# Reordering the opening norms of an attention and MLP kernel: tile 3's norm ahead of tile 4's statistics, half of tile 2's statistics between the first two norms

## The chip, the cores and the metric

The kernel runs on one core of one Trainium2 chip. The metric is the device time of one execution in microseconds (us). The span of a trace is some 1.8 us shorter than the time of the same execution.

## The reference, cut to what matters

```
x = A_x                                  # 2048 tokens x 1024, bf16
xn = layernorm(x)
s = attention(xn, wqkv, wo)              # 32 heads of 32
y = layernorm(xn)
g = silu(gelu(y @ w1 + b1) @ w2 + b2)
return x + s * g
```

The 2048 tokens are 16 tiles of 128. Below, PE is the engine for matmuls (TensorE), ACT is ScalarE, DVE is VectorE and POOL is GpSimd; PEld is PE's loading of weights. Before any matmul of use can start, a tile of `x` must be loaded, its mean and variance computed, the tile normalized, and the result transposed. The change concerns this opening alone.

## The kernel before

Every operation goes through a small helper, `op`, that records what it reads and writes and derives the semaphores. An engine executes its own operations in the order in which they were recorded, so the order of the calls below is the schedule.

```
load_x(0); load_x(1)
load_wq(0, (1,))                 # key weights, 512 KB
load_x(2); load_x(3)
load_wq(0, (0,))                 # query weights
load_x(4); load_x(5)
load_wq(0, (2,))                 # value weights
... the other tiles

def stat(tb):                    # DVE: two halves of 512 columns, then their merge
    bn_half(tb, 0); bn_half(tb, 1); bn_merge(tb)

def rstd(lo, hi):                # var + eps, then ** -0.5
    op("vector" if hi == 1 else "gpsimd", ... tensor_scalar(L(0), mv[:, lo:hi, 1], EPS, None, op0=ALU.add) ...)
    op("gpsimd", ... tensor_tensor(L(2), L(0), mhalf[:, 0:hi - lo], op=ALU.pow) ...)

def xnorm(tb): ...               # DVE: (x - mean) * rstd, 128x1024 bf16

def norm_pair(p):
    lo, hi = 2 * p, 2 * p + 2
    if p == 0:
        stat(0); rstd(0, 1)
        stat_scalar(1)           # tile 1's statistics, on ACT
        xnorm(0); xnorm(1)
        stat(2); rstd(2, 3)
        stat(3)
        xnorm(2)
        rstd(3, 4)
    elif p == 1:
        stat(4)
        xnorm(3)                 # tile 3's norm, behind tile 4's statistics
        stat(5); rstd(4, 6)
    else: ...                    # stat, two norms, stat, rstd
```

PE's order in the opening is: warm-up matmuls, transposes of tiles 0 and 1 (line L386), key and query matmuls of this first pair (L687), transposes of tiles 2 and 3, value matmuls of the first pair (L703), then the first scores (L867) and, on ACT, the first exponential (L879). A pair is two tiles, the first pair tiles 0 and 1. From the fourth pair on the transposes are done by DMA (tiles 6 to 15).

The softmax here doesn't subtract the row's maximum and nothing guards it: scores larger than these inputs give would overflow.

## Time and profile before

| | before |
|---|---|
| median of 6 runs | 1090.66 us (1089.76 to 1091.55) |
| profiled span | 1087.7 us |
| PE busy | 1077.0 us |
| first exponential starts | 16.19 us |
| first matmul of the body (L395) | 47.92 us |

These are two lines of the page of the kernel before, its busy time by engine and its chain of waits by engine:

```profile
PE 1077.0 (99%) x29156; PEld 700.9 (64%) x29156; DVE 627.3 (58%) x1395; ACT 1043.5 (96%) x1197; POOL 22.6 (2%) x70
PE 54%; ACT 44%; DVE 1%; DMA 0%; issue 0%; POOL 0%; SPq 0%
```

### The profile page before, as it was taken

What the parts mean: (1) busy time and instruction counts of PE and PEld (TensorE: products, weight loads), DVE (VectorE), ACT (ScalarE), POOL (GpSimd) and SP (SyncE); (2) the same over time, 40 slices, a digit from 0 to 9 for tenths busy, and PEclk for the clock granted to TensorE, in tenths of its full rate; (3) what the DMA queues carried; (4) which work ended last, traced back from release to release, by engine and by line L of the source; (5) the groups of instructions that cost most, each with busy time, mean ns of one, the idle gap of its engine ahead of it and who ended that gap; (6) DMA issues with size and microseconds to landing.
All of it is one profiled execution on the core that took longest, in us unless ns stands there. A gap on an engine that the chain in (4) does not pass through costs nothing.

```text
span 1087.7 us, 61820 instructions
## 1 busy us (share of the span) xinstructions
PE 1077.0 (99%) x29156; PEld 700.9 (64%) x29156; DVE 627.3 (58%) x1395; ACT 1043.5 (96%) x1197; POOL 22.6 (2%) x70
## 2 busy tenths in 40 slices
PE   8999999999999999999999999999999999999998
PEld 5766666666666666666666666666666666666665
DVE  7388843477732576642377743378733377635556
ACT  7899998999999999999999999999999999999993
POOL 4400000000000000000000000000000000000000
PEclk9999999999999999999999999999999999999999
DMA  8844365423364224345333264423254333675434
GB/s 247 169 139 137 111 172 149 121 61 110 109 164 122 65 63 120 109 104 148 90 100 100 69 161 119 125 81 109 81 132 119 91 119 108 198 201 107 108 92 124
DMA packets 209336, 131.92 MB, mean 121 GB/s; under 512 B 52538, under 2 KB 200250, under 8 KB 209082
## 3 DMA queue, kind: packets, MB, share of 16 engines
q1 hardware_dynamic: 209082, 127.97, 42.8%
q8 instruction: 228, 3.74, 1.4%
q14 instruction: 26, 0.21, 0.1%
HBM read 104.87 MB, written 12.06 MB: 107 GB/s over the span
## 4 chain that ended last, share of the span: by engine, by line
PE 54%; ACT 44%; DVE 1%; DMA 0%; issue 0%; POOL 0%; SPq 0%
ACT P L879 40%; PE ps L395 32%; PE ps L867 9%; PE ps L896 5%; PE ps L899 5%; ACT u L565 4%; PE ps L703 1%; PE ps L687 1%; ACT thz L609 0%; DVE stats L324 0%; DMA OT<-in_A_x_dram 0%; DVE wq L669 0%; PE ps L386 0%; DVE hT L359 0%; ACT hT L714 0%
## 5 line engine op out<-in xcount | busy, mean ns | idle before, releaser
L879 ACT ACTIVATE P<-ps 128x1024 bf16<-128x1024 f32 x1024 | 968.7, 1085 | 8.6 <-PE ps L867 4.0
L896 PE MATMUL ps<-P,VP 128*32 128x256 bf16 x4096 | 256.3, 273 | 0.0
L899 PE MATMUL ps<-P,ones 128*32 128x256 bf16 x4096 | 256.2, 273 | 0.0
L395 PE MATMUL ps<-yTc,war 128*32 128x352 bf16 (+1 forms) x5376 | 225.3, 309 | 0.0
L395 PE MATMUL ps<-hT,war 128*32 128x352 bf16 (+1 forms) x5376 | 225.2, 309 | 0.0
L867 PE MATMUL ps<-QT,KT 32*128 32x256 bf16 x4096 | 203.4, 273 | 2.9 <-ACT P L879 0.2
L395 PEld LDWEIGHTS ps<-hT,war 128*32 128x32 bf16 x5376 | 127.9, 96 | 73.9 <-issue 25.1
L395 PEld LDWEIGHTS ps<-yTc,war 128*32 128x32 bf16 x5376 | 127.4, 96 | 74.2 <-DVE xb L548 19.0
L867 PEld LDWEIGHTS ps<-QT,KT 32*128 32x128 bf16 x4096 | 60.7, 92 | 114.9 <-issue 60.0
L605 DVE TENSOR_SCALAR zh<-ps,b2h 128x352 f32<-128x352 f32 (+1 forms) x48 | 27.5, 572 | 182.3 <-PE ps L395 182.3
L571 DVE SCALAR_TENSOR_TENSOR hT<-u,xb 128x352 bf16<-128x352 f32 (+1 forms) x168 | 84.4, 510 | 68.4 <-ACT u L565 68.4
L548 DVE TENSOR_SCALAR xb<-ps,b1T 128x352 f32<-128x352 f32 (+1 forms) x168 | 96.3, 573 | 47.7 <-PE ps L395 42.8
L896 PEld LDWEIGHTS ps<-P,VP 128*32 128x32 bf16 x4096 | 109.1, 97 | 20.4 <-issue 1.3
L899 PEld LDWEIGHTS ps<-P,ones 128*32 128x32 bf16 x4096 | 109.2, 97 | 18.7
L395 PE MATMUL ps<-xnT,wq 128*32 128x352 bf16 (+1 forms) x2688 | 112.7, 309 | 0.0
L395 PEld LDWEIGHTS ps<-xnT,wq 128*32 128x32 bf16 x2688 | 63.7, 96 | 37.2 <-DVE xb L548 9.1
L558 DVE SCALAR_TENSOR_TENSOR u<-u,xb 128x352 f32<-128x352 f32 (+1 forms) x168 | 82.6, 510 | 1.9
L554 DVE TENSOR_TENSOR u<-xb 128x352 f32<-128x352 f32 (+1 forms) x168 | 82.6, 508 | 0.7
L565 ACT ACTIVATE u<-u 128x704 f32<-128x704 f32 (+1 forms) x84 | 71.9, 861 | 0.0
L395 PE MATMUL ps<-xnT,OT 128*32 128x352 bf16 (+2 forms) x1568 | 62.9, 306 | 0.2 <-DVE wq L669 0.2
L395 PE MATMUL ps<-wq,xnT 128*32 128x256 bf16 x1536 | 50.8, 274 | 0.0
L395 PEld LDWEIGHTS ps<-xnT,OT 128*32 128x32 bf16 x1568 | 37.7, 96 | 19.9 <-DVE wq L669 7.7
(61 smaller groups left out, 477.6 us busy)
## 6 DMA issues: line engine op xcount, KB each, us to landing
war<-in_B_w_dram SPq DMA_DIRECT2D x336, 256.0 KB, 3.3
wq<-in_A_wqkv_dram SPq DMA_DIRECT2D x36, 128.0 KB, 2.4
OT<-in_A_x_dram SPq DMA_DIRECT2D x16, 256.0 KB, 5.5
xnT<-in_A_x_dram SPq DMA_DIRECT2D x16, 256.0 KB, 3.2
out_dram<-wq SPq DMA_DIRECT2D x15, 256.0 KB, 2.0
y_scratch<-OT SPq DMA_DIRECT2D x14, 256.0 KB, 2.6
gT_scratch<-gst SPq DMA_DIRECT2D x32, 88.0 KB, 3.1
xnT<-in_A_wo_dram SPq DMA_DIRECT2D x8, 256.0 KB, 3.9
```

Source lines behind the costliest of these rows:

```text
L395: ins = e.matmul(outs(j), lhsT=lhs(j), rhs=rhs, start=start, stop=stop, tile_position=(0, 32 * j), skip_group_check=True)
L548: x0 = op("vector", lambda e: e.tensor_scalar(xb[:, 0:n], bank(bk, 0, n), b1T[:, f:f + 1], None, op0=ALU.add), r=[("b", bk), "b1"], w=[kx] ...
L554: x = op("vector", lambda e: e.tensor_tensor(ub[:, 0:n], xb[:, 0:n], xb[:, 0:n], op=ALU.mult), r=[kx], w=[ku], c=151 + 1.042 * n)
L558: x = op("vector", lambda e: e.scalar_tensor_tensor(ub[:, 0:n], ub[:, 0:n], 1.0 / 0.044715, xb[:, 0:n], op0=ALU.add, op1=ALU.mult), r=[kx, ...
L565: x = op("scalar", lambda e: e.activation(ut[:, :, 0:n], ut[:, :, 0:n], ACT.Tanh, scale=0.7978845608028654 * 0.044715), r=kus, w=kus, c=48 ...
L571: op("vector", lambda e: e.scalar_tensor_tensor(hT[:, fq, 0:n], ut[:, i, 0:n], 1.0, xq[:, 0:n], op0=ALU.add, op1=ALU.mult), r=[kus[i], kq] ...
L605: x0 = op("vector", lambda e: e.tensor_scalar(zh[:, 0:n], bank(bk, 0, n), 0.25, b2h[:, nb:nb + 1], op0=ALU.mult, op1=ALU.add), r=[("b", bk ...
L687: ins = e.matmul(bank(bk, off, off + 256), lhsT=wq[:, which, dc, 0:128], rhs=xnT[:, dc, t0:t0 + 256], start=dc == 0, stop=dc == DC - 1, sk ...
L867: ins = e.matmul(bank(bks[j], kh * 256, (kh + 1) * 256), lhsT=KT[i2][32 * j:32 * j + 32, k0:k0 + 128], rhs=QT[i2][32 * j:32 * j + 32, qb * ...
L879: op("scalar", lambda e, p=p, sl=sl: e.activation(pb[:, 2 * p:2 * p + 2, :, :].rearrange("p a b q -> p (a b q)"), ps[:, sl * 1024:(sl + 1) ...
L896: e.matmul(bankq(ACC, j, 0, QW), lhsT=VP[vp][:, kb, vo + 32 * j:vo + 32 * j + 32], rhs=pb[:, j, kh, :], start=first, stop=False, tile_posi ...
L899: ins = e.matmul(bankq(ACC, j, QW, 2 * QW), lhsT=ones[:, 0:32], rhs=pb[:, j, kh, :], start=False, stop=last, tile_position=(0, 32 * j), sk ...
```

## The change

The intent is to have tile 3 normalized before PE wants to transpose it. Tile 4's statistics move behind that norm. Half of tile 2's statistics fills a gap of DVE between norms 0 and 1, for which tile 2 has to be loaded earlier. A small step of tile 3's moves from GpSimd to DVE.

```diff
         load_x(1)
+        load_x(2)
         load_wq(0, (1,))
-        load_x(2)
         load_x(3)
...
-            op("vector" if hi == 1 else "gpsimd", ...
+            op("vector" if hi in (1, 4) else "gpsimd", ...
...
                 xnorm(0)
+                bn_half(2, 0)
                 xnorm(1)
-                stat(2)
+                bn_half(2, 1)
+                bn_merge(2)
                 rstd(2, 3)
                 stat(3)
+                rstd(3, 4)
                 xnorm(2)
-                rstd(3, 4)
+                xnorm(3)
             elif p == 1:
                 stat(4)
-                xnorm(3)
                 stat(5)
```

More of the change, by code (lines that the diff above doesn't have):

```diff
@@ L337, in rstd @@
             L = lambda k: lnp[:, k, lo:hi]
-            op("vector" if hi == 1 else "gpsimd", lambda e: e.tensor_scalar(L(0), mv[:, lo:hi, 1], EPS, None, op0=ALU.add),
+            op("vector" if hi in (1, 4) else "gpsimd", lambda e: e.tensor_scalar(L(0), mv[:, lo:hi, 1], EPS, None, op0=ALU.add),
                r=[("mv", t) for t in range(lo, hi)], w=[("l0", t) for t in range(lo, hi)], c=169.0)
```

## The prediction

> **What bounds the kernel now.** I began with the page: PE is busy for 1077.0 of 1087.7 us and ACT for 1043.5, and the chain that ended last is PE 54% and ACT 44%, DVE 1%. So nothing on DVE matters in the body of the kernel. The diff, however, only touches the prologue (loads, norms of tiles 0 to 3), and there the limits are different. So I read next the chain of waits in order of time from 0 to 60 us:
>
> ```profile
> 7.60 0.55 DVE hT L359
> 8.15 1.21 DVE stats L324 x2
> 9.35 0.02 issue
> 9.38 0.21 DVE mv L328
> 9.59 1.16 DVE stats L324 x2
> ...
> 10.98 0.41 DVE hT L359
> 11.39 1.21 DVE stats L324 x2
> 12.60 0.02 issue
> 12.62 0.21 DVE mv L328
> 12.83 0.42 DVE hT L359
> 13.25 0.05 issue
> 13.30 0.62 PE ps L386 x8
> 13.92 1.75 PE ps L703 x16
> 15.66 0.33 PE ps L867 x8
> ```
>
> Read it as one sentence: from 7.60 to 13.30 us the end of the kernel hangs on DVE, which does tile 1's norm, the statistics of tiles 2 and 3, tile 2's norm, **the statistics of tile 4**, and only then tile 3's norm; that releases tile 3's transposes on PE (L386), the value matmuls (L703) and the first scores (L867). From 13.30 to 56.3 us the chain stays on PE, then alternates with ACT. So a microsecond taken off before 13.30 should shift all that follows, unless something with its own clock (a load) comes in.
>
> How large is the hole? The timeline of PE, ACT and DVE from 10 to 16 us shows it. These are rows of that answer (start, us, engine and line, what; in brackets the idle time before and what ended it):
>
> ```profile
> 11.70 0.61 PE L386 MATMUL ps<-ident,hT 128*128 128x128 bf16 x8
> ...
> 11.90 0.38 ACT L693 ACTIVATE KT<-ps 128x256 bf16<-128x256 f32 x1 [2.01 <-PE ps L687]
> ...
> 12.18 0.38 ACT L693 ACTIVATE QT<-ps 128x256 bf16<-128x256 f32 x1
> ...
> 13.30 0.62 PE L386 MATMUL ps<-ident,hT 128*128 128x128 bf16 x8 [0.99 <-DVE hT L359]
> ```
>
> PE finished tile 2's transposes at 12.31, then sat 0.99 us until tile 3's norm. It is PE's only such gap after the key/query matmuls of the first pair began at 9.94. Its length caps most of what the change can win.
>
> **What the Trainium skill says.** (1) "Perfetto Trace Analysis", section "DMA Instruction — HWDGE (DVE, Sync)": a DMA's bar in the profile ends when the issuing sequencer is done; the movement is not in it. So I take starts plus the "to landing" figure, and the trace agrees: the 0.39 us bar of tile 0's load at 0.72 lands 2.9 later, 3.62, and DVE starts on it at 3.65. (2) "Runtime: NRT & Kernel Launch", section "Instruction fetch mechanics": instructions are refilled by DMA in blocks of 16 KiB, 256 instructions. The trace agrees: PE's 29156 + 29156 instructions over 256 are 227.8, and the page counts 228 packets in its "instruction" queue. (3) "DMA: Bandwidth & Descriptors", section "Queues, rings and completion order": each DMA engine takes turns between queues, and a load's completion needs every engine it uses. That makes rival B below possible. (4) "VectorE: DVE Perf Modes", section "The DRAIN you can't avoid": a DVE instruction is not free even where it waits for nothing. The trace agrees in kind: statistics of a tile take 1.32 us from start to start of the aggregation, that 0.12 more, a norm 0.41 to 0.46.
>
> **The change, part by part.** No arithmetic is added or removed, and PE and ACT keep their order.
> - *Tile 2's load ahead of the key weights.* Now tile 2 is issued at 2.11 and lands 5.6 later, 7.7 us. Put third, it follows tile 1 (landed 4.19) with 256 KB; the later 256 KB loads landed some 0.7 apart (7.7, 8.33), so I estimate 5.0. The key weights (issue 1.64 + 5.3 = 6.94 now) go to about 7.7. The query weights have the same bytes ahead of them as before: 3.21 + 6.6 = 9.81, against a use at 9.94. So the first matmuls stay at 9.94, but with only 0.13 to spare.
> - *Half of tile 2's statistics into the gap between norms 0 and 1.* DVE is idle for 1.00 us before 7.60, waiting for GpSimd's power of tile 1. Norm 0 starts at 6.06, so the half (0.66) can run from 6.5 to 7.2 with the load long there. It is free; norm 1 stays at 7.60. DVE is then 0.65 ahead.
> - *Tile 3's first scalar step on DVE instead of GpSimd.* 0.15 on DVE (the row of L338 on DVE) in place of 0.41 on GpSimd, which that instance took beside a DVE norm (0.22 elsewhere).
> - *Norm 3 ahead of the statistics of tile 4.* New DVE times: norm 1 7.60, second half 8.05, aggregation 8.71, statistics of tile 3 from 8.83, aggregation 10.10 to 10.31, scalar step to 10.50; GpSimd's power (0.56, starting 0.09 after) to 11.14. Norm 2 runs 10.45 to 10.95, norm 3 waits for the power, 11.17 to 11.67. That is 1.58 ahead of 12.75, of which PE can use less: PE is in the key/query matmuls until 11.66, so tile 2's transposes stay at 11.70, and tile 3's follow at once, at about 12.15 (a pair of tiles takes 0.89 on the chain, one 0.45) in place of 13.30.
> - *The next limit.* The value matmuls now start at 13.75. They could start at 12.60, but need the value weights (issue 6.25 + 6.4 = 12.65) and a bank that the query copy leaves at 12.56. So about 12.70: **a gain of 1.05 us**, and the first scores at 14.55.
> - *Given back on DVE.* The 0.3 us that DVE waits for the power before norm 3 and the 0.12 of the scalar step come off its lead, so statistics of tile 5 end only some 0.2 us earlier than now, and so do norms 4 and 5 (15.78 and 16.2, against 15.98). PE wants them at 16.5 and 17.0: they still fit. All later norms are also only 0.2 earlier, while PE wants them 1.05 earlier.
>
> Sum, if nothing else intervenes: 1090.87 - 1.05 = 1089.8.
>
> **Rivals.**
> A, *the gain passes through whole*. For it: each later unit of the prologue is 4.48 us on PE, ACT has 0.38 spare in each, and DVE needs only 3.7 per unit. Transposed tiles 6 and 7 land at 23.0 and 24.4, for a use at 24.9; tiles 14 and 15 at 42.2, for one at 42.9. 1089.8.
> B, *a transpose by DMA takes over*. Tile 9's was issued at 25.19 and took 5.1 to landing, where others take 2.7 to 3.9, so it landed at 30.3; PE took the data at 30.43:
>
> ```profile
> xnT<-hT SPq DMA_TRANSPOSE x1, 5.1
> ```
> ```profile
> PEld ps L687 <- DMA xnT<-hT: 0.2, 1, 0.2
> ```
> The reason is in the packets: at 27.55 one 16 KB instruction fetch lay in front of the last part of this transpose on one engine, and that engine trickled until 29.3 at 10 GB/s. Its norm comes only 0.2 earlier after the change. If the landing stays at 30.1, unit 4 starts no earlier than 30.2 and nearly all is lost: 1090.6. Against it: the fetch follows PE's own progress, so it should come 1.05 earlier too, at 26.5, where it still meets this transpose; I expect part of the delay to move with it, and a loss of 0 to 0.8.
> C, *the load order costs something*: query weights after 9.94 would push PE's first pair and subtract one for one. Same bytes ahead of them, so I give it 0.1 on average.
> D, *nothing follows, because the body is bound elsewhere*. The chain after 56 us alternates PE and ACT with no wait on a load that has its own clock (loads are issued behind PE), so a shift should last to the end. The instruction order of later DVE work is fixed by a timing model inside the kernel's builder; a shift of its start can swap a few of them, some tenths either way.
>
> **Range and chances.** A gets about 45%, B 45% with a mean loss of 0.5, the rest small: an expected gain of 0.75 us, 1090.1. The three runs before span 1.8 us, so medians differ by some 0.6 by chance alone; with B's spread that gives 1089.0 to 1091.1 for 8 in 10. 2% is 22 us, more than the whole stretch between 7.6 and 30 us; neither a win nor a loss of that size has a source here: 0.01 each.
>
> **What would show it.** Right: no gap on PE at 12.3; tile 3's transposes near 12.15, value matmuls near 12.7, first scores near 14.5, first exponential near 15.1 in place of 16.19; one half statistic on DVE between the first two norms; norm 3 waiting about 0.3 for GpSimd. For B: a gap on PE before the key matmuls of unit 4 at 29.4, with a DMA as releaser. Wrong: PE's first key matmuls later than 9.94, tile 2's half still waiting for its load at 6.5, norms 4 or 5 holding PE at 16.5, or a start of the body (the first L395, 47.92 now) earlier by one microsecond with an end that is not.

## The result, and the profile after

The changed kernel took 1089.78 us (median of 6 runs, 1088.58 to 1090.78), the kernel before 1090.66 in the same rounds. The ratio is 0.999 with a 95% interval of 0.9977 to 1.0003. Ratios are the mean time of one kernel's fast runs over the mean of the other's of the same rounds, so not quite the ratio of the medians. By times alone the gain isn't separated from zero. The traces separate it in the opening. PE and ACT execute the same sequence in both kernels, and DVE does from tile 5's statistics on, so each step of one trace can be set against the same step of the other.

The two lines of the page that answer to those of before:

```profile
PE 1077.7 (99%) x29156; PEld 701.4 (65%) x29156; DVE 627.6 (58%) x1396; ACT 1043.6 (96%) x1197; POOL 22.5 (2%) x69
PE 57%; ACT 42%; DVE 0%; DMA 0%; issue 0%; POOL 0%; SPq 0%
```

DVE's share of the chain went from 1% to 0%. The chain of waits in order of time (start, duration, what) shows where it went:

```profile
7.52 0.56 DVE hT L359
...
8.12 0.62 PE ps L386 x8
8.74 1.08 PE ps L758 x5
...
9.86 1.92 PE ps L687 x16
11.78 0.89 PE ps L386 x16
...
12.68 1.92 PE ps L703 x16
14.60 0.33 PE ps L869 x8
```

The chain leaves DVE with norm 1, at 8.07 instead of 13.25, and the transposes of tiles 2 and 3 follow each other as one block of 16. The lines are numbered two higher from L756 on, as the changed kernel has two lines more.

DVE's own timeline (the kernel after; in brackets the idle time before an instruction and what ended it):

```profile
6.29 0.69 DVE L324 BATCH_NORM_STATS2 stats<-OT 128x6 f32<-128x512 bf16 x1
7.52 0.55 DVE L359 TENSOR_SCALAR hT<-OT,mv,lnp 128x1024 bf16<-128x1024 bf16 x1 [0.54 <-POOL lnp L717]
...
10.33 0.15 DVE L338 TENSOR_SCALAR lnp<-mv 128x1 f32<-128x1 f32 x1
10.40 0.54 DVE L359 TENSOR_SCALAR hT<-OT,mv,lnp 128x1024 bf16<-128x1024 bf16 x1
11.39 0.55 DVE L359 TENSOR_SCALAR hT<-OT,mv,lnp 128x1024 bf16<-128x1024 bf16 x1 [0.45 <-POOL lnp L340]
...
16.08 0.96 DVE L359 TENSOR_SCALAR hT<-OT,mv,lnp 128x1024 bf16<-128x1024 bf16 x2
```

The half of tile 2's statistics (6.29) sits in the gap and still leaves 0.54 us of it. Norm 3 (11.39) follows norm 2, with 0.45 us of waiting for GpSimd's power. Norms 4 and 5 (16.08) come no earlier than before (15.98).

What PE waits for next is in the weight load ahead of the value matmuls:

```profile
12.68 1.64 PEld L703 LDWEIGHTS ps<-wq,xnT 128*128 128x128 bf16 x16 [0.18 <-DMA wq<-in_A_wqkv_dram]
```

The value weights, landed at 12.64, are the new limit. First exponential 15.13 (before 16.19), body start 46.86 (before 47.92): 1.06 us earlier, both.

Set against the trace before, exponential by exponential, this lead is 1.06 us without a change from 14.6 to 418 us. Between 418 and 426 us it falls to 0.62, and from 438 us to the end it is 0.76, which is the difference of the two spans but for rounding (1087.7 - 1086.9). So 0.3 us was lost in the body. There PE stopped in the middle of one item:

```profile
417.24 0.73 PE L395 MATMUL ps<-yTc,war 128*32 128x320 bf16 x16 [0.51 <-issue]
```

PE's releaser is not named ("issue"), and no semaphore of a load is waited for there: PE first waits for the weights that were being loaded then at 423.7. The place of the stop tells what it was. As the prediction read from the packet count, PE's instructions come by DMA in fetches of 256, each one packet of the "instruction" queue. Counted in PE's instructions from the start of the trace (matmuls, weight loads and semaphore waits), the stop lies after 21441, which is 83 x 256 + 193, and 83 fetches had begun by then. The last of them had begun at 413.87, 1.8 us after PE passed the place 256 instructions earlier (the median over all traces is 0.6), and took 1.90 us (median 1.03). PE went on 1.47 us after its end.

The same count fits every stop of PE over 0.22 us between 60 and 1000 us in the 14 traces: 12 of 12 lie 193 or 194 past a multiple of 256, always with the block of the last begun fetch next. And at the 2898 such places behind the 20th fetch, PE never went on sooner than 1.1 us after the end of that fetch; counted one instruction earlier, it did so 24 times. So PE was out of instructions. Below this is called a fetch stop.

### The profile page after: what moved, and what is told of

Same layout as the page of the kernel before. It is cut to its first block, busy times and chain, and to the rows that moved or that the text cites. A ratio compares the mean times of both kernels' runs of the same rounds, so it can differ in the third digit from the quotient of the medians.

```text
span 1086.9 us, 61820 instructions
## 1 busy us (share of the span) xinstructions
PE 1077.7 (99%) x29156; PEld 701.4 (65%) x29156; DVE 627.6 (58%) x1396; ACT 1043.6 (96%) x1197; POOL 22.5 (2%) x69
## 3 DMA queue, kind: packets, MB, share of 16 engines
HBM read 104.87 MB, written 12.06 MB: 108 GB/s over the span
## 4 chain that ended last, share of the span: by engine, by line
PE 57%; ACT 42%; DVE 0%; DMA 0%; issue 0%; POOL 0%; SPq 0%
ACT P L881 38%; PE ps L395 33%; PE ps L869 9%; PE ps L898 6%; PE ps L901 6%; ACT u L565 3%; PE ps L687 1%; PE ps L703 1%; ACT thz L609 0%; DMA OT<-in_A_x_dram 0%; PE ps L386 0%; DVE wq L669 0%; ACT hT L714 0%; DVE zh L605 0%; DVE wq L671 0%
## 5 line engine op out<-in xcount | busy, mean ns | idle before, releaser
L395 PE MATMUL ps<-yTc,war 128*32 128x352 bf16 (+1 forms) x5376 | 225.5, 309 | 0.5 <-issue 0.5
L395 PE MATMUL ps<-hT,war 128*32 128x352 bf16 (+1 forms) x5376 | 225.3, 309 | 0.0
L395 PEld LDWEIGHTS ps<-yTc,war 128*32 128x32 bf16 x5376 | 127.4, 96 | 74.9 <-DVE xb L548 19.2
L395 PEld LDWEIGHTS ps<-hT,war 128*32 128x32 bf16 x5376 | 127.9, 96 | 73.9 <-issue 25.1
L395 PE MATMUL ps<-xnT,wq 128*32 128x352 bf16 (+1 forms) x2688 | 112.7, 309 | 0.0
L395 PEld LDWEIGHTS ps<-xnT,wq 128*32 128x32 bf16 x2688 | 63.7, 96 | 37.2 <-DVE xb L548 9.1
L395 PE MATMUL ps<-xnT,OT 128*32 128x352 bf16 (+2 forms) x1568 | 62.9, 306 | 0.2 <-DVE wq L669 0.2
L395 PE MATMUL ps<-wq,xnT 128*32 128x256 bf16 x1536 | 50.8, 274 | 0.0
L395 PEld LDWEIGHTS ps<-xnT,OT 128*32 128x32 bf16 x1568 | 37.7, 96 | 19.9 <-DVE wq L669 7.7
```

The lines of the kernel that those rows point to most:

```text
L395: ins = e.matmul(outs(j), lhsT=lhs(j), rhs=rhs, start=start, stop=stop, tile_position=(0, 32 * j), skip_group_check=True)
```

## The experiments

Theory S, behind the prediction: each part of the change frees DVE time ahead of tile 3's norm, and PE's need caps the sum at 1.06 us. Rival O: the order of the norms does everything, and the load and the half are idle extras. Two more questions are what the instruction fetch does (rival B of the prediction), and what the body does with the lead. "Body start" below is the first L395. Experiments e1 to e5 and f3 are single executions of unknown state (e3 and e5 twice); the granted clock was 0.999 or 1.000 in each trace. Only steps of their traces are compared, not their times (1089.1 to 1091.3 us).

**e1: the order alone.**

```diff
                 stat(3)
+                rstd(3, 4)
                 xnorm(2)
-                rstd(3, 4)
+                xnorm(3)
             elif p == 1:
                 stat(4)
-                xnorm(3)
                 stat(5)
```

> Kernel before with one thing of the change: tile 3's power and norm ahead of tile 4's statistics (loads as before, statistics of tile 2 in one piece, scalar step of tile 3 on GpSimd). Theory S (each part frees DVE time, PE's need caps the sum at 1.06): norm 3 at about 12.15 (GpSimd's two steps end only then), tile 3's transposes 12.7, value matmuls at 13.1, first L395 of the body at 47.3, so 0.6 of the 1.06 us. Rival O (the order alone does everything, load and half are idle extras): value matmuls at 12.7, body 1.06 earlier.

Measured: norm 3 at 12.28, value matmuls at 13.34, body start 47.70. That is 0.41 us ahead at the value matmuls, and only 0.22 ahead at the body. Two rows of DVE (e1), norm 3 and norms 4 with 5:

```profile
12.28 0.55 DVE L359 TENSOR_SCALAR hT<-OT,mv,lnp 128x1024 bf16<-128x1024 bf16 x1 [0.84 <-POOL lnp L340]
...
16.97 0.97 DVE L359 TENSOR_SCALAR hT<-OT,mv,lnp 128x1024 bf16<-128x1024 bf16 x2
```

The order alone makes DVE stand for 0.84 us before norm 3, waiting for GpSimd, and everything behind it pays: norms 4 and 5 come 1.0 us later than in the kernel before (15.98), so the transposes of tiles 4 and 5 move only from 17.68 to 17.54. Rival O falls, and theory S, which expected 0.6 at the body, overlooked this cost. By the fifth pair the lead is down to 0.22 us: its key matmuls start at 30.21, just after tile 9's transpose landed at 30.16.

**e2: the load and the half alone.**

```diff
+        load_x(2)
         load_wq(0, (1,))
-        load_x(2)
...
                 xnorm(0)
+                bn_half(2, 0)
                 xnorm(1)
-                stat(2)
+                bn_half(2, 1)
+                bn_merge(2)
```

> Kernel before with the other part: tile 2's load third and half of its statistics between norms 0 and 1; norm 3 stays behind tile 4's statistics. Theory S: all of DVE 0.65 to 0.7 us earlier from norm 2 on, norm 3 at 12.1, transposes 12.6, value matmuls 13.05, body start about 0.65 to 0.7 earlier than before. Rival O: body start unchanged (within 0.1).

Measured: value matmuls at 13.43, body start 47.59, a lead of 0.32 and 0.33 us. Half of what was expected, for a reason that I hadn't seen: tile 4's statistics were now ahead of their own data. The rows of DVE (e2):

```profile
10.97 1.29 DVE L324 BATCH_NORM_STATS2 stats<-OT 128x6 f32<-128x512 bf16 x2 [0.21 <-DMA OT<-in_A_x_dram]
...
12.42 0.49 DVE L359 TENSOR_SCALAR hT<-OT,mv,lnp 128x1024 bf16<-128x1024 bf16 x1
```

Norm 2 came 0.62 us earlier (10.27), norm 3 only 0.33, as tile 4 landed at 10.95 in this execution. The two parts alone add up to 0.22 + 0.33 = 0.55 at the body, together they give 1.06. But part of e2's shortfall is chance of this execution. In the first trace of the changed kernel tile 4 landed at 10.48; with that, its statistics could have begun at 10.68 (norm 2 at 10.27 plus 0.41) in place of 10.97, and e2's lead would be about 0.6 and the sum about 0.8. This is an estimate. What remains is shown by e1: alone, the order makes DVE wait for GpSimd, and the half of the statistics pays for that wait. The order also takes norm 3 out from behind tile 4's load where that is late.

**e3: the scalar step back on GpSimd, twice.**

```diff
-            op("vector" if hi in (1, 4) else "gpsimd", ...
+            op("vector" if hi == 1 else "gpsimd", ...
```

> Changed kernel with tile 3's scalar step back on GpSimd. Theory S: the step takes 0.4 there, beside norm 2, so norm 3 starts at about 11.5 in place of 11.39 and ends at 12.0, still ahead of PE's need at 12.15: value matmuls stay at 12.68, body start within 0.1 of the changed kernel's 46.86. Rival (norm 3 is the bound in the changed kernel): value matmuls later by the same 0.1 to 0.3.

> Tile 3's scalar step on GpSimd again: in the first run of it norm 3 came at 11.68 and tile 3's transposes at 12.28, but the value weights landed at 13.2 (12.6 to 12.8 in most runs) and held PE. With weights landing by 12.7 the value matmuls start at 12.7 to 12.8, 0.1 at most behind the changed kernel's, and body start at 46.9 to 47.0: the scalar step's place is worth at most 0.1. Rival: they start at 13.2 again although the weights are there.

Measured: norm 3 at 11.68 and 11.75, 0.3 later than in the changed kernel, tile 3's transposes at 12.28 and 12.35. The value matmuls came at 13.25 and 13.32, but in both executions they waited for the value weights, which landed at 13.2 and 13.3 (body start 47.42 and 47.49). The question is therefore not answered by a run. Worked out: a block of eight transposes takes 0.45, so with weights at 12.64, as in the changed kernel, PE could have gone on at 12.28 + 0.45 = 12.73, against 12.68. That the step's place is worth under 0.1 us is an estimate, and holds only where the weights land no earlier than that.

**e4: tile 2's load back behind the key weights, the half still in the gap.**

```diff
-        load_x(2)
         load_wq(0, (1,))
+        load_x(2)
```

> Changed kernel with tile 2's load back behind the key weights, the half of its statistics still between norms 0 and 1. The load lands at 7.67, so DVE would hold norm 1 behind it: half 7.7 to 8.35, norm 1 at 8.3 in place of 7.52, first key matmuls at about 10.65 in place of 9.86, body start about 47.6, 0.75 later than the changed kernel and 0.3 earlier than before. Rival (the load's place does not matter): norm 1 at 7.5 and body start 46.9.

Measured, from the rows of DVE (e4):

```profile
7.94 0.69 DVE L324 BATCH_NORM_STATS2 stats<-OT 128x6 f32<-128x512 bf16 x1 [1.52 <-DMA OT<-in_A_x_dram]
8.55 0.53 DVE L359 TENSOR_SCALAR hT<-OT,mv,lnp 128x1024 bf16<-128x1024 bf16 x1
```

DVE is in order, so it stood 1.52 us for tile 2, with tile 1's norm ready behind it. Norm 1 moved from 7.52 to 8.55, the first key matmuls from 9.86 to 10.88, body start to 47.80: 0.94 later than the changed kernel and 0.12 ahead of the kernel before. The load's place is needed, and it cost 0.2 more than expected because the load landed at 7.92.

**f3: the same warm-up in more instructions.** PE warms up with 13 matmuls of 512 columns. Cut into 52 of 128, it has as many columns, but 78 more instructions (39 matmuls, 39 weight loads), so later instruction fetches come earlier.

```diff
-            for i in range(k):
-                ins = e.matmul(bank(0), lhsT=ident[:], rhs=cold, ...)
+            parts = 4 if k == 13 else 1
+            w = 512 // parts
+            for i in range(k * parts):
+                ins = e.matmul(bank(0, 0, w), lhsT=ident[:], rhs=cold[:, 0:4 // parts, :], ...)
```

> Changed kernel; the 13 warm-up matmuls of 512 columns cut into 52 of 128, so 78 more PE instructions in the same PE time. Theory of the fetch (16 KB instruction fetches follow PE's instruction count and hold back one engine's share of the transpose that is under way): the second fetch comes 3 us earlier, at about 22.7 in place of 25.74, into tile 7's transpose (22.9 to 23.9), which then lands at 26 to 26.7 in place of 24.5; PE waits for it ahead of the key matmuls of the fourth pair (24.9 otherwise) for 1 to 1.8 us, and the body starts that much later than 46.86. Rival (fetches don't matter, late landings are chance): tile 7 lands at 24.5, no gap, body start 46.9.

Measured: the opening matched the changed kernel (value matmuls 12.59), and then PE stopped ahead of the fourth pair's key matmuls, as expected, though for less time:

```profile
25.34 1.92 PE L687 MATMUL ps<-xnT,wq 128*128 128x256 bf16 x16 [0.49 <-DMA xnT<-hT]
```

The fetch came at 20.87, earlier than expected, and met tile 6's transpose: that landed at 23.77 (23.11 in the changed kernel), tile 7's behind it at 25.29 (24.52). Body start 47.30, 0.44 later than the changed kernel. Nothing else was altered. This one execution isn't alone: of the transposes of tiles 6 to 9 in all 14 traces, the 24 that had a PE fetch begin while they were under way took 3.51 to 5.11 us from issue to landing, the other 32 took 2.70 to 2.87. Tile 6 met a fetch in f3 only (3.51, against 2.81 to 2.82 in the other 13), and there tiles 8 and 9, which a fetch delays in the changed kernel (4.20 and 3.73), took 2.70 and 2.80. So the position of the fetch moves the landing of a transpose and, where that is near PE's need, PE.

**e5: the value weights ahead of tile 5, twice.**

```diff
-        load_x(5)
         load_wq(0, (2,))
+        load_x(5)
```

> Changed kernel with the value weights' load ahead of tile 5's. Theory: in the changed kernel the value matmuls at 12.68 wait for these weights (landing 12.64) and for nothing later than 12.5; with the weights at about 11.95 they start at 12.5, body start 46.7, 0.15 us earlier. Tile 5's load lands 1.5 later (12.6), still ahead of its statistics at 13.29. Rival: no change, because the query copy or the transposes end at the same time.

> Value weights ahead of tile 5's load again: in the first run of it tile 2's load came 1.5 us late on one engine and held norm 1. If tile 2 lands by 6.3 this time: value weights at about 12.0, value matmuls at 12.5, body start 46.7. If loads are late again: as in the first run, no gain.

A miss, both times. Tile 2 landed at 7.0 in both, the value weights only at 12.8, and the value matmuls started at 12.89 and 12.84. Norm 3 was late too (11.83 and 11.76, behind tile 2), so tile 3's last transposes started only at 12.84 and 12.77, and weights and transposes were ready together. Body start was 47.49 and 47.45, as PE also waited for tile 9's transpose by DMA (the first execution; 0.30 in the second):

```profile
30.01 1.92 PE L687 MATMUL ps<-xnT,wq 128*128 128x256 bf16 x16 [0.27 <-DMA xnT<-hT]
```

This is rival B of the prediction, in a kernel that is close to the changed one: tile 9 landed at 29.96 and 29.92. The new order didn't make tile 2 late: the load that was moved ahead, the value weights, was issued only at 7.21 and 7.17, after tile 2 had landed. Whether it helps when the early loads are on time stays untested.

**The two kernels again.** No edit.

> The changed kernel again, unchanged, with five rounds. Prologue theory: first exponential 1.06 us before that of the kernel before, exactly as in the first profile, and first L395 at 46.9. Body theory N (the 0.3 us that were lost in the body near 417 us were chance: one piece of weights whose last sixteenth came 2 us after the others behind an instruction fetch): no such loss at that place this time, but losses of some tenths at other places. Rival C (the change causes it): the same PE gap of 0.5 us near 417 us again. Ratio: 0.9990, plus or minus 0.001.

> The kernel before again, for a second trace. Theory N: prologue the same within 0.1 us (first L395 at 47.9), body longer or shorter by some tenths, by PE gaps at places where the first trace had none. Rival C: the body is the same within 0.1.

> The changed kernel once more, beside the run above. Prologue: first exponential 0.95 to 1.1 us ahead of the kernel before, body start 46.8 to 47.0. Theory T: if the gate's load lands within 4.2 us there is no PE gap near 957, if it takes over 5 there is one. Times 1088.6 to 1091, median 1089.5.

| execution (trace) | tile 2 landed | value weights landed | value matmuls | body start | span |
|---|---|---|---|---|---|
| before | 7.67 | 12.61 | 13.75 | 47.92 | 1087.7 |
| before, again | 7.83 | 12.78 | 13.80 | 47.96 | 1088.2 |
| after | 5.50 | 12.64 | 12.68 | 46.86 | 1086.9 |
| after, again | 6.23 | 12.75 | 12.80 | 46.97 | 1087.6 |
| after, third | 7.40 | 13.86 | 13.91 | 48.08 | 1090.9 |

Times: 1089.36 us against 1090.46 (ratio 0.9994, interval 0.9981 to 1.0008) in the second set of rounds, 1090.67 against 1091.20 (0.9996, 0.9983 to 1.0008) in the third. Over all three sets (16 runs of the changed kernel, 24 of the kernel before) the means are 0.74 us apart, with a 95% interval of about 0.1 to 1.4. This is worked out from the listed times without regard to the sets. The repeat gave the lead in the opening again (0.95 us at the body against the first trace of the kernel before, 0.99 against the second). The third was a miss (a lead of 0.95 to 1.1 and a median of 1089.5 had been expected). It lost all of the lead in the opening, and its rows of DVE and PE say why:

```profile
7.42 0.69 DVE L324 BATCH_NORM_STATS2 stats<-OT 128x6 f32<-128x512 bf16 x1 [0.94 <-DMA OT<-in_A_x_dram]
8.03 0.53 DVE L359 TENSOR_SCALAR hT<-OT,mv,lnp 128x1024 bf16<-128x1024 bf16 x1
```

```profile
13.91 1.92 PE L703 MATMUL ps<-wq,xnT 128*128 128x256 bf16 x16 [0.49 <-DMA wq<-in_A_wqkv_dram]
```

In that execution 15 of the 16 DMA engines had delivered tile 2 at 5.53, the last at 7.40, and the value weights came at 13.86. The half of the statistics stood in front of norm 1 and passed the delay on (as in e4), and the value matmuls waited for the weights. The weights decided it: the last transposes of tile 3 started at 13.20, so PE could have gone on at about 13.25. The changed kernel has tied the first pair to two loads that the kernel before needed later.

The body: the gap near 417 us was gone in the repeat, so the part of the expectation that called it chance held. It lost 0.75 us of its lead elsewhere, near 957 us. This PE gap was in neither trace of the kernel before nor in the first of the changed one (after, again):

```profile
957.04 0.59 PE L395 MATMUL ps<-hT,war 128*32 128x320 bf16 x11 [0.33 <-issue]
```

It is a fetch stop (200 x 256 + 193 instructions). Its fetch began 2.8 us after PE had passed the place 256 instructions earlier; in the four traces without a loss here (the two of the kernel before, the first of the changed one, e2) the same fetch began 1.0 to 1.5 us after, in the nine with a loss 1.9 to 3.4. The nine are the repeat, the third (about 1 us lost) and all of e1, e3, e4, e5 and f3, seven traces that lost 0.5 to 1.6 us between 945 and 965 us.

What made the fetch late there isn't shown. The first transposed load of the gate for the output stage is issued a little earlier, and was suspected when g3 was planned. It landed 5.4 us after its issue in the repeat, 6.2 in the third and 5.0 to 5.8 in six of the seven, against 3.9 to 4.4 in the four without a loss. But the second of e3 lost 0.5 us with 4.3. Whether the opening was early or late showed no effect.

The body of the kernel before isn't free of this either: its second trace lost 0.47 us against the first, in fetch stops at 440 and 809 us. The third of the changed kernel lost 3.0 us after the opening, 2.8 of it at seven such places.

**g3: that one load behind the weights.** The changed kernel, with the first gate load kept back until the second group of weights is queued. In its place the queue issues a later tile's load of `x`, so two loads change places; each engine's order is else the same.

```diff
-            i = 0 if tag is None else next((i for i, z in enumerate(due) if z[2] == tag), None)
+            ok = (lambda z: z[2][0] != "gres" or cnt["piece"] >= NPC - 2) if tag is None else (lambda z: z[2] == tag)
+            i = next((i for i, z in enumerate(due) if ok(z)), None)
```

> Changed kernel with one DMA moved: the first transposed load of the gate for the output stage (issued near 949.5 us in between two groups of weights) goes behind the second group. Theory T (the PE gap near 957 us, present in 6 of 10 traces, comes in those where that load takes 5.4 to 5.8 us to land and the weights behind it are late): no gap near 957 in this trace; of the five times none above about 1090.0, median 1088.9, 0.5 below the changed kernel's. Rival U (the gap has another cause): gap of 0.3 to 1.2 us there in this trace with better than even chance, times spread over 2 us as before.

Measured: 1090.23 us (1089.70 to 1090.85), against 1091.20 for the kernel before and 1090.67 (1090.12 to 1092.65) for the changed kernel in the same rounds. The ratio to before is 0.9989 (0.9976 to 1.0003). The gap near 957 us isn't in its trace, though the fetch for that place still began 2.3 us after PE passed the one before. Between 961 and 981 us it lost 0.94 us (from 0.40 ahead of the kernel before to 0.54 behind) in small steps, the largest around a 0.23 us PE gap at 975.66, with the third group of weights issued only from 968.96. The stops at 961.5, 975.7 and 980.4 are at block ends again, so here too PE waited for instructions. The wait moved more than it went. The medians are 0.44 apart, the expected 0.5, but the expected level (1088.9) and ceiling (1090.0) did not hold: the whole set of rounds was slower. I don't claim that it beats the changed kernel.

## Why the prediction was right or wrong

The prediction was right: 1089.78 us lies in its range, 0.3 below its centre. That alone says little, as the kernel before (1090.66) lies in the range too and single runs vary by 2 us. What supports it is the opening, step by step:

- **What bounds the opening.** Right. Norm 3 left the chain, the 0.99 us gap of PE is gone, and the lead at the body is 1.06 us where 1.05 was worked out, with the value weights as the next limit. e1, e2 and e4 show that the parts depend on each other.
- **Tile 2's load at 5.0.** Landed at 5.50, 6.23 and 7.40 in three executions. The estimate took the bytes ahead of it and left out that the last of 16 engines can come up to 1.9 us after the rest. Of the ten executions that load tile 2 third (experiments included), it landed by 5.5 in three and at 6.2 to 7.4 in seven, so "with the load long there" was too sure. Norm 1 came at 7.48 to 7.59 in eight of them and at 7.72 and 8.03 in two.
- **"Only 0.13 to spare" for the query weights.** Wrong. PE does eight key matmuls first, 0.9 us, and the query weights are read after them. In e3 they landed at 10.40 and the key matmuls started at 9.85 with no wait. No run bears rival C out.
- **Norm 3 at 11.17.** It was 11.39. The power took 0.78 instead of 0.56, since it ran beside norm 2 on DVE: in all eight traces where it did, it took 0.78 to 0.79, and alone or beside statistics 0.56 to 0.57. The page "SBUF — State Buffer" of the Trainium skill, section "Terms", says that DVE and GpSimd take turns for one pair of ports, held for a whole instruction; the trace agrees in direction, 0.21 us more for an overlap of 0.37. PE wanted the norm at 12.06, so it cost nothing.
- **Norms 4 and 5 "0.2 earlier".** They were 0.1 later (16.08), by this 0.2 and the scalar step, which cost DVE 0.19 in place of 0.12 (norm 2 started 0.31 after the start of the aggregation, 0.12 before the change). The conclusion held: transposes at 16.64 and 17.10, no wait.
- **Rival A or B.** A in the first trace and the repeat: tile 9 landed at 29.01 and 29.12 (30.29 before), and the fifth pair started at 29.37 and 29.49, no gap. The fetch came at 25.74 (26.5 was expected) and met tile 8's transpose instead. A margin of some 0.3 us decided it (in e5 PE went on 0.05 us after the landing); in e5 B came true with 0.3 us, and in f3 its mechanism with 0.5 on another tile. One reading for B was wrong: "others take 2.7 to 3.9" holds for tiles 6 to 11 of that trace, but tiles 12 to 15 took 4.1 to 5.4.
- **Rival D, "a shift should last to the end".** Too simple. The chain has no wait on a load there, as the prediction read, but PE also waits for its own instructions, which the profile's page doesn't name ("issue"). In fetch stops the body gives lead back in some executions (0.3, 0.84 and 3.0 us in the three of the changed kernel). In the repeat this brought about the prediction's own last sign of being wrong: the body started 0.95 us earlier, the end came 0.1 earlier (0.6 against the second trace of the kernel before). That this is a price of the change isn't shown; places and sizes differ between executions of one kernel, and the kernel before lost 0.47 in one of its two traces. How often each kernel pays is open.

Open: why loads come late on their last DMA engine in some executions (no instruction fetch of any engine lies between 0 and 13 us in any trace, so early loads don't wait for one), what makes PE's fetches late, and how often the changed kernel loses its lead to either.

## What to carry to other kernels

When an engine works in order, ask of each operation that you bring forward what it now stands in front of, and when its data comes: a piece put into a free gap is free only if its load is there, with its spread. Two reorderings can look worse alone than they are together, because one hides behind a wait that the other removes, so test them together as well. A stop of PE that no semaphore explains is worth a count of its instructions. And where the gain is below the spread of the times, compare step by step in traces, and in more than one execution.

## What the Trainium skill lacked or had wrong

- "Runtime: NRT & Kernel Launch", section "Instruction fetch mechanics", calls the cost of crossing a block boundary mostly hidden. At most crossings that holds here, but PE stood 0.23 to 0.95 us in 12 fetch stops among some 2900 crossings, and it never went on sooner than 1.1 us after the end of a fetch. The page doesn't say that a fetch holds back other traffic either: 24 transposes with a fetch under way landed 3.51 to 5.11 us after issue, 32 without took 2.70 to 2.87.
- "DMA: Bandwidth & Descriptors", section "Why a DMA increments its semaphore by 16 and not by 1", explains that a load is complete only with its last engine, but gives no spread (another section calls two of the engines usually slower, without a figure). Here a 256 KB load was there on 15 engines at 5.53 us and on the sixteenth at 7.40, and a weight piece at 415.31 and 417.33.
- No page that I found has a duration for GpSimd's power on one column: 0.56 to 0.57 us alone or beside DVE statistics, 0.78 to 0.79 beside a DVE norm.
